# Mish MLP behind attention and soft MoE: the first chunks in another order, w_out tiles converted between the last expert products

## The chip, the cores and the metric

One core of one Trainium2 chip runs the whole program. The metric is the device time of one execution in microseconds; the kernel before takes 648.38 us, the median of three runs (647.77 to 648.62).

## The reference, cut to what matters

```python
x = attention(q, k, v, p)                      # [4608, 512], through 32 packed tokens per head
logits = x @ phi                               # soft MoE, 8 experts of 4 slots
slot_in = softmax(logits, 0).T @ x
slot_out[e] = relu(slot_in[e] @ w1[e]) @ w2[e] # 32 slots x 512
x = softmax(logits, 1) @ slot_out              # [4608, 512]
h = x @ w_in                                   # w_in [512, 2048]
out = (h * tanh(softplus(h))) @ w_out          # Mish; w_out [2048, 512]
```

Since x of the last layer is C @ slot_out, with C of 4608 x 32, the kernel never forms x: it forms slot_out @ w_in (32 x 2048, called MS) and then h = C @ MS.

## The kernel before, in words

Three stages follow each other: attention, the eight experts (weights streamed from HBM), and the MLP. The change lies where the experts end and the MLP begins, some 217 to 275 us after the start.

The helper names: `so` is the PSUM bank that collects the expert products; `ex_o(7, ...)` (L1009) adds those of the last expert. Its transpose `SOT` (128 x 4 x 32) is built through `so_sb` (two half copies, VectorE L1393 and ScalarE L1401) and `sot_ps` (L1394 to L1410) and copied out at L1414.

w_in and w_out arrive as 64-bit numbers and are converted on chip. For each of 16 `w_out` tiles of 128 x 512: `cz(k)` is a ScalarE pass over the high words (L280 or L282) into a `w64` buffer (four of them in turn), `cu(k)` two VectorE passes for the first four tiles (L286 and L289) and three for the others (L286, L289, L293). The tile is then split in two halves for the fast matmul format: `whi`, a rounding copy on ScalarE (L300 or L1183), and `wlo`, the rest, by a subtraction: on GpSimd for tiles 0 to 3 (`cw`, L301), on VectorE for tiles 4 to 15 (`cl`, L1184). Their loads wait in SyncE's queue (L174), in the order of a list made by `plan()`; a load into a ring slot waits until the slot's last user is done.

MS is made in four column groups of 512: `emit_mp(n)` multiplies SOT by a quarter of w_in (L1146) and copies the product to `msb` (L1149); `emit_mr(n)` repeats it over the four partition groups with one matmul (L1154), copies it to MS on an engine named in the call (L1156) and subtracts on VectorE, for partitions 64 to 127, what the rounded copy already holds (L1157). That subtraction reads the PSUM tile of the matmul once more. In the kernel before the tiles of `emit_mp` and `emit_mr` come from the pools `ps_x` (three banks) and `ps_so` (one).

The MLP goes over token blocks n of 256 and chunks c of 512 hidden columns. For a step (n, c): `emit_h(n, c, z)`, z = 0 and 1, makes half of h by two matmuls (L1199) into a tile of the pool `ps_h`, and ScalarE applies Mish (L1204). `emit_c` makes `gh` (rounding copy, ScalarE L1223) and `gl` (rest, VectorE L1224). `emit_o` issues 24 matmuls (L1317): 12 into a bank X for the first 128 tokens, and 12 into a bank Y; each dozen is gh by whi, gh by wlo, gl by whi, four each. Between the dozens it calls `mid`, which issues `emit_h` of the step after next. Column group c of MS serves chunk c. The first eight steps alternate two blocks: (0,0), (1,0), (0,1), (1,1), (0,2), (1,2), (0,3), (1,3).

`ps_h` has two buffers of two banks each, given out in turn, and a new tile may be written when the users of the tile that had the buffer are done:

```python
ps_h = hp_ctx.enter_context(tc.tile_pool(name="ps_h", bufs=2, space=PSUM, reuse_waits="tile"))
hp = ps_h.tile([128, 2, 512], F32, name="h3", tag="hp")[:, 0]      # in emit_h, one for each z
```

Nothing is scheduled by a planner here: each engine works through its instructions in the order in which the program text issues them, so a waiting instruction holds up all behind it on its engine. In the loop, step i issues, in this order: `emit_c` of step i+1; `emit_o` with `mid` in its middle; `cl` of two tiles, `cu` of the next two, `cz` of the two after those.

Of the kernel before, what the change touches and what calls it, by code (L numbers as in the profile page):

```python
# [19 lines left out]
def kernel(  # L20
# [264 lines left out]
    def cv_u(nm, i, name, dst, z, tv, fold):  # L285
        nc.vector.tensor_scalar(out=tv[:, :, 0], in0=tv[:, :, 0], scalar1=29, scalar2=None, op0=ALU.logical_shift_right)  # L286

    def cv_m(nm, i, name, dst, z, tv, fold):
        nc.vector.scalar_tensor_tensor(  # L289
            out=z if fold else tv[:, :, 1], in0=z, scalar=3, in1=tv[:, :, 0], op0=ALU.logical_shift_left, op1=ALU.bitwise_or,  # L290
        )
        if not fold:
            nc.vector.scalar_tensor_tensor(  # L293
                out=z, in0=z, scalar=-(2 ** 31), in1=tv[:, :, 1], op0=ALU.bitwise_and, op1=ALU.bitwise_or,
            )
        done(*name)

    def cv_w(nm, ft, name, w, z, tv, fold):

        nc.scalar.copy(out=whi[:, ft], in_=w)  # L300
        nc.gpsimd.tensor_tensor(out=wlo[:, ft], in0=w, in1=whi[:, ft].bitcast(F32), op=ALU.subtract)  # L301

    bgq = []

# [670 lines left out]
    def warm(n):  # L975

        if n:
            ps = ps_x.tile([128, 512], F32, name="warm", tag="x")
        for _ in range(n):
            nc.tensor.matmul(ps[:, 0:256], lhsT=ident, rhs=win[0][:, 0:256], start=True, stop=True)  # L980
# [28 lines left out]
    def ex_o(e, n=FT1, w=0, lo=0):  # L1009
        h1T = ex[e][1]  # L1010
        for ft in range(lo, n):
            g = ft % 4
            nc.tensor.matmul(
                so[32 * g:32 * g + 32], lhsT=h1T[:, ft], rhs=take("w2", e, ft // 2)[:, (ft % 2) * DM:(ft % 2 + 1) * DM],
                start=(e == 0 and ft < 4), stop=(e == E - 1 and ft >= n - 4),
            )
            if ft % 2:
                done("w2", e, ft // 2)
                if ft < n - 1:
                    warm(w)  # L1020
# [98 lines left out]
    ex_x(7)  # L1119
    ex_o(6)  # L1120
    combine_t(Lc[1], 7)
    warm(2)
    ex_o(7, FT1 - 2, 1)
    zero_c = two.tile([1, 128], F32, name="zero_c", tag="Lr")
    nc.gpsimd.memset(zero_c, 0.0)
    late_w = {}
# [8 lines left out]
    def ps_m():  # L1135
        np[0] += 1
        return ps_x.tile([128, 512], F32, name="mp", tag="x") if np[0] % 4 else ps_so.tile([128, 512], F32, name="so")

    def emit_mp(n, copy, i=0, w=512):

        mp = ps_m()
        if not i:
            msb[n] = t2.tile([128, 512], F32, name="msb", tag="msb")
        for kt in range(4):
            c = 512 * (kt % 2) + i
            nc.tensor.matmul(  # L1146
                mp[32 * kt:32 * kt + 32, 0:w], lhsT=SOT[:, kt], rhs=win[2 * n + kt // 2][:, c:c + w], start=True, stop=True,
            )
        copy(out=msb[n][:, i:i + w], in_=mp[:, 0:w])  # L1149

    def emit_mr(n, copy, i=0, w=512):

        mr = ps_m()
        nc.tensor.matmul(mr[:, 0:w], lhsT=idrep, rhs=msb[n][:, i:i + w], start=True, stop=True)  # L1154
        dst = MS[:, 512 * n + i:512 * n + i + w]
        copy(out=dst, in_=mr[:, 0:w])  # L1156
        nc.vector.tensor_tensor(out=dst[64:128], in0=mr[64:128, 0:w], in1=dst[64:128].bitcast(F32), op=ALU.subtract)  # L1157
# [13 lines left out]
    def cz(k):  # L1171
        late_w[k] = cv_z(*AFTER[E - 1, 1][k], fold=k < 4)
# [2 lines left out]
        cv_u(*late_w[k])  # L1175
        cv_m(*late_w[k])

    def cw(k):
        cv_w(*late_w[k])

    def cl(k):
        w, ft = late_w[k][3], late_w[k][1]
        nc.scalar.copy(out=whi[:, ft], in_=w)  # L1183
        nc.vector.tensor_tensor(out=wlo[:, ft], in0=w, in1=whi[:, ft].bitcast(F32), op=ALU.subtract)  # L1184

    R = {}

# [30 lines left out]
    def emit_c(n, c):  # L1218

        s, S = blk.pop(("m", n, c))  # L1220
        gh, gl = (wg.tile([128, 1024], F32, name=x, tag="wg").bitcast(F32R).rearrange("p (f n) -> p f n", f=4) for x in ("gh", "gl"))
        if S is None:
            nc.scalar.copy(out=gh, in_=s)  # L1223
            nc.vector.tensor_tensor(out=gl, in0=s, in1=gh.bitcast(F32), op=ALU.subtract)  # L1224
            blk["g", n, c] = gh, gl
            return
        Sh, Sl = (g2.tile([128, 1024], F32, name=x, tag=x, bufs=2).bitcast(F32R).rearrange("p (k f n) -> p k f n", k=4, f=2) for x in ("Sh", "Sl"))
        blocks = ((slice(0, 4), slice(0, 128)), (slice(2, 4), slice(128, 256)))
        for f, t in blocks:
            nc.scalar.copy(out=gh[:, f, t], in_=s[:, f, t])  # L1230
        nc.scalar.copy(out=Sh, in_=S)  # L1231
        for f, t in blocks:
            nc.vector.tensor_tensor(out=gl[:, f, t], in0=s[:, f, t], in1=gh[:, f, t].bitcast(F32), op=ALU.subtract)  # L1233
        nc.vector.tensor_tensor(out=Sl, in0=S, in1=Sh.bitcast(F32), op=ALU.subtract)  # L1234
        blk["g", n, c] = gh, gl, Sh, Sl
# [124 lines left out]
    def emit_store(n):  # L1360
# [24 lines left out]
        else:  # L1385
            for tt in range(2):
                for z in range(2):
                    b = 4 * (n - TB // 2) + 2 * tt + z
                    for j in range(2):
                        p0 = 64 * z + 32 * j  # L1390
                        (nc.scalar if n == NBLK - 1 and j else nc.sync).dma_start(out=rows(b)[:, 16 + j], in_=osb[p0:p0 + 32, tt])

    nc.vector.tensor_copy(out=so_sb[:, 0:256], in_=so[:, 0:256])  # L1393
    nc.tensor.matmul(sot_ps.rearrange("p k m -> p (k m)"), lhsT=zero_c, rhs=zero_c, start=True, stop=False)  # L1394
    for kt in range(4):
        i = 0 + 128 * kt
# [2 lines left out]
            start=False, stop=False,  # L1399
        )  # L1400
    nc.scalar.copy(out=so_sb[:, 256:512], in_=so[:, 256:512])  # L1401
    cz(0)
    for kt in range(4):
        nc.tensor.matmul(sot_ps[:, kt], lhsT=so_sb[:, 128 * kt:128 * kt + 128], rhs=ids, start=False, stop=False)
    for kt in range(4):
# [3 lines left out]
            start=False, stop=(kt == 3),  # L1409
        )  # L1410
    done("w2", E - 1, 3)
    cv_u(*late_w[0])
    cz(1)
    nc.vector.tensor_copy(out=SOT, in_=sot_ps)  # L1414
    ep.close()
    W3 = arena.tile([128, 1024 * RW], F32R, name="W3", tag="AW")
# [8 lines left out]
        i = (0 if x == "osb" else 2048) + 1024 * turn[x]  # L1425
        return AY[:, i:i + 1024]

    cv_m(*late_w[0])
    emit_mp(0, nc.scalar.copy, 0, 256)
    emit_mp(0, nc.vector.tensor_copy, 256, 256)  # L1430
    cv_u(*late_w[1])
    emit_mp(1, nc.scalar.copy, 0, 256)
    cz(2)
    emit_mr(0, nc.scalar.copy, 0, 256)
    emit_mr(0, nc.scalar.copy, 256, 256)
    emit_mp(1, nc.vector.tensor_copy, 256, 256)
    cz(3)
    nc.scalar.activation(out=tab_c, in_=half_c, func=AF.Mish)
    cv_m(*late_w[1])
    cv_u(*late_w[2])  # L1440
    emit_mp(2, nc.scalar.copy)
    emit_mr(1, nc.vector.tensor_copy)
    cv_m(*late_w[2])
    emit_h(0, 0, 0)
    cw(0)
    cw(1)
    emit_h(0, 0, 1)
    cu(3)
    cw(2)
    emit_c(0, 0)  # L1450
    emit_mp(3, nc.vector.tensor_copy)
    emit_mr(2, nc.scalar.copy)
    cw(3)
    cz(4)
    emit_h(1, 0, 0)
    emit_h(1, 0, 1)
    cu(4)
    emit_mr(3, nc.scalar.copy)
    cz(5)
    cz(6)  # L1460
    cu(5)
    cz(7)
    R["X"], R["Y"] = (ps_x.tile([128, 512], F32, name="o3", tag="x") for _ in range(2))
    R["X1"], R["Y1"] = ps_x.tile([128, 512], F32, name="o3", tag="x"), ps_so.tile([128, 512], F32, name="so")
    work = {}
    for i, (n, c) in enumerate(steps):
        if i == 6:
            next(work[3])
            wp.close()
            g2 = ctx.enter_context(tc.tile_pool(name="g2", bufs=2, reuse_waits="tile"))  # L1470
            hp_ctx.close()
            ps_b = ctx.enter_context(tc.tile_pool(name="ps_b", bufs=1, space=PSUM, reuse_waits="tile"))
            R.update({x: ps_b.tile([128, 512], F32, name="o3", tag=x) for x in "ZV"}, U=R["X1"], W=R["Y1"])
        nx = steps[i + 2] if i + 2 < len(steps) else None
        last_s = fast(n, c) and c == ORDER[n][-1]

        def mid(z):
            if z == 0 and last_s:
                nc.scalar.copy(out=quads(n)[1], in_=rq("Z"))
            if z == 1 and last_s:  # L1480
                add(quads(n)[2], quads(n)[1], rq("V"))
            if z in (0, 2) and nx:
                emit_h(*nx, z // 2)

        if i + 1 < len(steps):
            emit_c(*steps[i + 1])
        emit_o(n, c, mid)
        early = c == ORDER[n][-1] and n + 1 in PLAIN and not fast(n + 1, ORDER[n + 1][0])
        if early and last_s:
            emit_store(n)  # L1490
        if nx:
            emit_m(*nx)
        if i < 6:
            for k in (2 * i + 4, 2 * i + 5):
                cl(k)
            for k in (2 * i + 6, 2 * i + 7):
                if k < NL:
                    cu(k)
            for k in (2 * i + 8, 2 * i + 9):
                if k < NL:  # L1500
                    cz(k)
        if i == 4:
            work.update({c: build_t(c, [late_w[k][3] for k in range(12, 16)] if c == 3 else None) for c in range(4)})
        if c == ORDER[n][-1] and not (early and last_s):
            emit_store(n)
        for x in TW.get(i, ""):
            next(work[int(x)])
# [31 lines left out]
```

## Time and profile before

| | |
|---|---|
| median of 3 runs | 648.38 us |
| the profiled execution's own time | 644.71 us |
| its span | 642.9 us |
| TensorE matmul busy | 611.3 us, 95% |
| VectorE, ScalarE, GpSimd busy | 501.1, 337.8, 55.2 us |
| mean granted TensorE clock | 0.989 |
| read from HBM, written | 79.2 MB, 9.4 MB |

The span is what the trace covers; the profiled execution's own time is 1.8 us more, for what lies around it. The median of the runs is 3.7 us above the profiled execution. A matmul's end is modelled, and matmuls overlap in the records, so the starts of TensorE's instructions say more than their sums. Times in the rows are counted from the start of the span.

### The profile page before, as it was taken

How to read it: one execution, taken by the hardware profiler on the slowest of the kernel's cores; microseconds unless marked ns; L12 is line 12 of the kernel's file. 1: busy time of each engine (PE TensorE's matmuls, PEld its weight loads, DVE VectorE, ACT ScalarE, POOL GpSimd, SP SyncE). 2: the span in 40 equal slices, each digit the busy share in tenths (PEclk: the TensorE clock that was granted, in tenths of full speed). 3: DMA queues.
4: the chain of work that ended last, by engine and by line, in shares of the span. 5: the costliest groups of instructions: out<-in, count | busy, mean ns of one | idle time of the engine just before them, and what ended most of it. 6: DMA issues, size and time to landing. Idle time of an engine off the chain costs nothing.

```text
span 642.9 us, 14422 instructions
## 1 busy us (share of the span) xinstructions
PE 611.3 (95%) x5874; PEld 528.6 (82%) x5874; DVE 501.1 (78%) x997; ACT 337.8 (53%) x681; POOL 55.2 (9%) x78
## 2 busy tenths in 40 slices
PE   7899999998998969999999999999999999999996
PEld 5777777776344548888899999999999999999996
DVE  5998888887564398988779987788778877887883
ACT  3345555646334367655456555555555555555551
POOL 5122222121020030010000000000000000000000
PEclk9899999998999979999999999999999999999999
DMA  8988955999999960020110110111011101110111
GB/s 283 344 292 292 343 174 199 405 413 396 360 410 412 412 223 1 1 53 14 33 34 2 34 34 2 35 34 34 2 34 34 34 2 34 34 34 2 34 34 34
DMA packets 42354, 89.61 MB, mean 139 GB/s; under 512 B 10928, under 2 KB 19248, under 8 KB 42288
## 3 DMA queue, kind: packets, MB, share of 16 engines
q1 hardware_dynamic: 41840, 88.36, 38.8%
q8 instruction: 46, 0.75, 0.5%
q10 hardware_dynamic: 192, 0.26, 0.2%
q14 instruction: 20, 0.16, 0.1%
q0 software_dynamic: 256, 0.07, 0.0%
HBM read 79.23 MB, written 9.44 MB: 138 GB/s over the span
## 4 chain that ended last, share of the span: by engine, by line
PE 65%; DVE 18%; DMA 8%; ACT 5%; issue 1%; SPq 1%; DVEq 0%; POOL 0%; ACTq 0%; POOLq 0%
PE o L1317 39%; PE so L1317 14%; DMA AW<-in_moe_w_dram 6%; PE h L1199 5%; DVE kT L335 4%; DVE A L507 1%; DMA r_wo<-in_moe_w_out_dram 1%; DVE mx L506 1%; PE s L487 1%; DVE AY L1358 1%; DVE S L1215 1%; DVE sm L522 1%; DVE nmx L383 1%; PE s L820 1%; ACT AT L545 1%
## 5 line engine op out<-in xcount | busy, mean ns | idle before, releaser
L1317 PE MATMUL o<-W,gh 128*128 128x256 f32 (+1 forms) x888 | 159.4, 306 | 0.5 <-DVE AY L1358 0.5
L1317 PEld LDWEIGHTS o<-W,gh 128*128 128x128 f32 x888 | 129.7, 190 | 10.0 <-issue 1.9
L1230 ACT CAST gh<-AY 128x512 fp32r<-128x512 f32 x116 | 53.8, 511 | 109.1 <-PE o L1317 109.1
L1204 ACT ACTIVATE AY<-h 128x512 f32<-128x512 f32 x132 | 77.1, 594 | 37.4 <-PE h L1199 36.0
L1317 PE MATMUL o<-W,gl 128*128 128x256 f32 (+1 forms) x444 | 94.3, 302 | 0.0
L1233 DVE TENSOR_TENSOR gl<-AY,gh 128x512 fp32r<-128x512 f32 x116 | 59.4, 553 | 33.0 <-ACT gh L1230 33.0
L1234 DVE TENSOR_TENSOR Sl<-S,Sh 128x1024 fp32r<-128x1024 f32 x58 | 70.9, 1223 | 10.4 <-ACT Sh L1231 9.0
L1317 PEld LDWEIGHTS o<-W,gl 128*128 128x128 f32 x444 | 70.7, 188 | 4.5
L1317 PE MATMUL o<-T,Sh 128*128 128x256 f32 x464 | 73.9, 281 | 0.4 <-DVE AY L1358 0.4
L1231 ACT CAST Sh<-S 128x1024 fp32r<-128x1024 f32 x58 | 60.8, 1049 | 5.6 <-DVE S L1215 4.3
L1317 PEld LDWEIGHTS o<-T,Sh 128*128 128x128 f32 x464 | 62.8, 189 | 0.6 <-DVE AY L1358 0.6
L1215 DVE TENSOR_TENSOR S<-AY 128x256 f32<-128x256 f32 x116 | 48.7, 420 | 9.9 <-ACT AY L1204 9.9
L1199 PE MATMUL h<-CS,W 128*128 128x256 f32 x288 | 55.7, 284 | 0.0
L1317 PE MATMUL o<-T,Sl 128*128 128x256 f32 x232 | 46.6, 282 | 0.0
L1199 PEld LDWEIGHTS h<-CS,W 128*128 128x128 f32 x288 | 43.9, 188 | 2.2 <-issue 0.7
L1358 DVE TENSOR_TENSOR AY<-AY,o 128x256 f32<-128x256 f32 x86 | 33.0, 417 | 9.4 <-PE o L1317 6.4
L1317 PE MATMUL so<-T,Sh 128*128 128x256 f32 (+1 forms) x232 | 38.7, 289 | 0.4 <-DVE AY L1358 0.4
L373 PE MATMUL s<-kT,win 128*128 128x288 f32 x128 | 34.7, 416 | 2.4 <-ACT win L385 2.3
L1317 PEld LDWEIGHTS o<-T,Sl 128*128 128x128 f32 x232 | 35.8, 190 | 0.0
L487 PE MATMUL s<-win,qT 128*128 128x128 f32 x256 | 33.7, 287 | 1.9 <-ACT win L353 1.9
L487 PEld LDWEIGHTS s<-win,qT 128*128 128x128 f32 x256 | 31.4, 200 | 2.8 <-issue 2.0
L1317 PEld LDWEIGHTS so<-T,Sh 128*128 128x128 f32 x232 | 32.5, 190 | 1.2 <-issue 0.6
(282 smaller groups left out, 1039.5 us busy)
## 6 DMA issues: line engine op xcount, KB each, us to landing
AW<-in_moe_w_dram SPq DMA_DIRECT2D x45, 512.0 KB, 10.2
r_wo<-in_moe_w_out_dram SPq DMA_DIRECT2D x16, 512.0 KB, 9.0
out_dram<-AY SPq DMA_DIRECT2D x64, 128.0 KB, 2.1
r_wi<-in_moe_w_in_dram SPq DMA_DIRECT2D x13, 512.0 KB, 8.8
AW<-in_q_dram SPq DMA_DIRECT2D x11, 576.0 KB, 5.2
AW<-in_k_dram SPq DMA_DIRECT2D x9, 576.0 KB, 7.3
AW<-in_v_dram SPq DMA_DIRECT2D x40, 128.0 KB, 5.6
AC<-in_moe_w_dram SPq DMA_DIRECT2D x10, 512.0 KB, 9.1
```

What stands on the lines that cost most here:

```text
L335: nc.vector.transpose(out=T[:, dh, main].rearrange("p (i r a) -> p a i r" if nm == "k" else "p (i a r) -> p a i r", i=4, a=4,), in_=x[:, 0 ...
L373: nc.tensor.matmul(ps[:, n, 0:288], lhsT=pBD[b % 2][:, hq, dh], rhs=kT[:, dh, 288 * n:288 * n + 288], start=(dh == 0), stop=(dh == 1),)
L487: nc.tensor.matmul(ps[:, k - lo], lhsT=d["qT", hq][:, dh, 64 + 128 * i:192 + 128 * i], rhs=ppBD[b % 2][:, hq, dh], start=(dh == 0), stop=( ...
L1199: nc.tensor.matmul(hp[:, 256 * f:256 * f + 256], lhsT=MS[:, 128 * ft:128 * ft + 128], rhs=CS[:, 256 * n:256 * n + 256], start=True, stop=True,
L1204: nc.scalar.activation(out=s, in_=hp.rearrange("p (f n) -> p f n", f=2), func=AF.Mish)
L1215: nc.vector.tensor_tensor(out=S[:, k], in0=x, in1=y, op=op)
L1230: nc.scalar.copy(out=gh[:, f, t], in_=s[:, f, t])
L1231: nc.scalar.copy(out=Sh, in_=S)
L1233: nc.vector.tensor_tensor(out=gl[:, f, t], in0=s[:, f, t], in1=gh[:, f, t].bitcast(F32), op=ALU.subtract)
L1234: nc.vector.tensor_tensor(out=Sl, in0=S, in1=Sh.bitcast(F32), op=ALU.subtract)
L1317: nc.tensor.matmul(o, lhsT=lhsT, rhs=rhs, start=first, stop=stop)
L1358: add = lambda o, x, y: nc.vector.tensor_tensor(out=o, in0=x, in1=y, op=ALU.add)
```

## The change

`warm(2)` and the call of `ex_o` for the last expert are taken from their place, and the call stands later, without the warming matmuls between its pairs, behind the conversion of w_out tile 0. The conversions of tiles 0 to 2 and `cz(3)` stand between the steps that build SOT, and the load of ScalarE's Mish table with them. `cw`, GpSimd's subtraction, is gone: `cwh(k)` is its ScalarE copy and `cwl(k)` the subtraction, on VectorE. Only column group 0 of MS is made ahead of the first h; two single matmuls (`fill`) into a spare tile stand between its parts. Group 1's product is made before the loop; its spreading and groups 2 and 3 are issued in `mid` of steps 0, 1 and 2, into the two banks of one `ps_h` tile for each step. In step 0, `emit_c` of step 1 and `emit_h` of step 2 stand behind `emit_o`. `cu(5)`, `cz(6)` and `cz(7)` move into step 0.

```diff
-    def cv_w(nm, ft, name, w, z, tv, fold):
-        nc.scalar.copy(out=whi[:, ft], in_=w)
-        nc.gpsimd.tensor_tensor(out=wlo[:, ft], in0=w, in1=whi[:, ft].bitcast(F32), op=ALU.subtract)
...
-    warm(2)
-    ex_o(7, FT1 - 2, 1)
...
-        mp = ps_m()
+        mp = ps_m() if n < 2 else hp_m[n]
...
-        mr = ps_m()
+        mr = ps_m() if n < 1 else hp_m[n + 4]
...
+    def cwh(k):
+        nc.scalar.copy(out=whi[:, late_w[k][1]], in_=late_w[k][3])
+    def cwl(k):
+        w, ft = late_w[k][3], late_w[k][1]
+        nc.vector.tensor_tensor(out=wlo[:, ft], in0=w, in1=whi[:, ft].bitcast(F32), op=ALU.subtract)
...
+    cz(0)
+    cu(0)
+    ex_o(7, FT1 - 2, 0)
+    cz(1)
     nc.vector.tensor_copy(out=so_sb[:, 0:256], in_=so[:, 0:256])
+    cu(1)
...
     nc.scalar.copy(out=so_sb[:, 256:512], in_=so[:, 256:512])
-    cz(0)
+    cz(2)
+    cu(2)
+    cz(3)
+    nc.scalar.activation(out=tab_c, in_=half_c, func=AF.Mish)
...
+    def fill(ps, n):
+        for _ in range(n):
+            nc.tensor.matmul(ps[:, 0:256], lhsT=ident, rhs=win[0][:, 0:256], start=True, stop=True)
+    cwh(0)
     emit_mp(0, nc.scalar.copy, 0, 256)
     emit_mp(0, nc.vector.tensor_copy, 256, 256)
+    cwh(1)
+    spare = ps_h.tile([128, 2, 512], F32, name="spare", tag="hp")
+    fill(spare[:, 0], 1)
     emit_mr(0, nc.scalar.copy, 0, 256)
     emit_mr(0, nc.scalar.copy, 256, 256)
+    fill(spare[:, 1], 1)
+    cwh(2)
     emit_h(0, 0, 0)
     emit_h(0, 0, 1)
     cu(3)
...
+    for f in (0, 2):
+        nc.scalar.copy(out=gh[:, f:f + 2], in_=s0[:, f:f + 2])
+    cwh(3)
+    for k in range(4):
+        cwl(k)
+    nc.vector.tensor_tensor(out=gl, in0=s0, in1=gh.bitcast(F32), op=ALU.subtract)
+    emit_mp(1, nc.scalar.copy)
     emit_h(1, 0, 0)
     emit_h(1, 0, 1)
+    cz(4)
     cu(4)
     cz(5)
...
-            if z in (0, 2) and nx:
+            if z == 0 and i < 3:
+                t = ps_h.tile([128, 2, 512], F32, name="mr", tag="hp")
+                hp_m.update({i + 5: t[:, 0], i + 2: t[:, 1]})
+                emit_mr(i + 1, nc.scalar.copy)
+                if i < 2:
+                    emit_mp(i + 2, nc.scalar.copy)
+            if z in (0, 2) and nx and i:
                 emit_h(*nx, z // 2)
-        if i + 1 < len(steps):
+        if i + 1 < len(steps) and i:
             emit_c(*steps[i + 1])
         emit_o(n, c, mid)
+        if not i:
+            emit_c(*steps[1])
+            for z in range(2):
+                emit_h(*nx, z)
+            for k in (5, 6):
+                cu(k) if k < 6 else cz(k)
+            cz(7)
```

## Rows read from the trace of the kernel before

**Rows 1.** Windows: busy us (instructions) of each engine, granted clock, DMA share, GB/s.

```profile
234.00:240.00 6.00, 5.88 (x12) 3.98 (x13) 5.46 (x10) 3.62 (x6) 0.47 (x1) 0.51 0.43 159
252.00:258.00 6.00, 6.00 (x29) 4.95 (x28) 5.82 (x10) 4.34 (x7) 0.00 (x0) 1.00 0.00 0
```

**Rows 2.** Timeline of TensorE: start, us, engine, line, operation, tiles, shape, count.

```profile
220.56 1.50 PE L1146 MATMUL mp<-win,SOT 128*32 128x256 f32 x24 [0.38 <-DVE SOT L1414]
...
226.22 1.06 PE L1146 MATMUL mp<-AY,SOT 128*32 128x512 f32 x8
227.22 1.12 PE L1154 MATMUL mp<-msb,idrep 128*128 128x512 f32 x2
...
234.12 2.07 PE L1154 MATMUL mp<-msb,idrep 128*128 128x512 f32 x2 [5.30 <-DVE msb L1149]
235.20 4.40 PE L1317 MATMUL o<-W,gh 128*128 128x512 f32 x8
...
240.54 0.64 PE L1199 MATMUL h<-CS,W 128*128 128x256 f32 x4
...
249.88 2.03 PE L1317 MATMUL o<-W,gh 128*128 128x512 f32 x8
...
252.68 0.62 PE L1199 MATMUL h<-CS,W 128*128 128x256 f32 x4
...
274.12 2.03 PE L1317 MATMUL o<-W,gh 128*128 128x512 f32 x8
```

**Rows 3.** The chain of waits, 227 to 232 us: start, us, what.

```profile
227.31 1.80 DVE w L289
...
230.64 1.57 DVE w L289
```

**Rows 4.** Windows of half a microsecond, TensorE alone: busy, granted clock, DMA.

```profile
233.00:233.50 0.50, 0.00 (x0) 0.51 0.82 82
239.50:240.00 0.50, 0.50 (x3) 0.66 0.27 107
```

**Rows 5.** Loads of w_out: the first and the fourth issue, and the time to landing.

```profile
206.90 0.33 SPq L174 DMA_DIRECT2D r_wo<-in_moe_w_out_dram  x1
210.81 0.33 SPq L174 DMA_DIRECT2D r_wo<-in_moe_w_out_dram  x1
...
r_wo<-in_moe_w_out_dram SPq DMA_DIRECT2D x1, 512.0 KB, 8.9
```

**Rows 6.** Timeline of ScalarE.

```profile
217.80 1.22 ACT L280 ACTIVATE w<-r_wo 128x512 f32<-128x512 f32 x2
221.26 0.37 ACT L1149 COPY msb<-mp 128x256 f32<-128x256 f32 x1 [2.25 <-PE mp L1146]
224.21 1.28 ACT L1438 ACT_TABLE_LOAD   x1
...
253.10 1.09 ACT L1204 ACTIVATE s<-h 128x512 f32<-128x512 f32 x2 [1.47 <-PE h L1199]
254.07 1.14 ACT L1183 CAST W<-w 128x512 fp32r<-128x512 f32 x2
...
256.65 1.04 ACT L1223 CAST gh<-s 128x1024 fp32r<-128x1024 f32 x1
```

**Rows 7.** Timeline of VectorE.

```profile
220.21 0.29 DVE L1414 COPY SOT<-sot_ps 128x128 f32<-128x128 f32 x1 [2.44 <-PE sot_ps L1407]
...
236.88 0.69 DVE L1157 TENSOR_TENSOR W<-mp,W 64x512 fp32r<-64x512 f32 x1
...
251.68 0.42 DVE L286 TENSOR_SCALAR r_wo<-r_wo 128x512 int32<-128x512 int32 x1
252.13 0.69 DVE L289 SCALAR_TENSOR_TENSOR r_wo<-w,r_wo 128x512 int32<-128x512 int32 x1
...
253.47 1.22 DVE L1224 TENSOR_TENSOR gl<-s,gh 128x1024 fp32r<-128x1024 f32 x1
254.73 1.29 DVE L1184 TENSOR_TENSOR W<-w,W 128x512 fp32r<-128x512 f32 x2
```

More of the change, by code (lines that the diff above doesn't have):

```diff
@@ L1137, in ps_m @@
         return ps_x.tile([128, 512], F32, name="mp", tag="x") if np[0] % 4 else ps_so.tile([128, 512], F32, name="so")
+    hp_m = {}
     def emit_mp(n, copy, i=0, w=512):
-        mp = ps_m()
+        mp = ps_m() if n < 2 else hp_m[n]
         if not i:
@@ L1176, in cu @@
         cv_m(*late_w[k])
-    def cw(k):
-        cv_w(*late_w[k])
+    def cwh(k):
[3 more added lines that the diff above has]
+        nc.vector.tensor_tensor(out=wlo[:, ft], in0=w, in1=whi[:, ft].bitcast(F32), op=ALU.subtract)
     def cl(k):
-        w, ft = late_w[k][3], late_w[k][1]
-        nc.scalar.copy(out=whi[:, ft], in_=w)
-        nc.vector.tensor_tensor(out=wlo[:, ft], in0=w, in1=whi[:, ft].bitcast(F32), op=ALU.subtract)
+        cwh(k)
+        cwl(k)
     R = {}
@@ L1411 @@
     done("w2", E - 1, 3)
-    cv_u(*late_w[0])
-    cz(1)
     nc.vector.tensor_copy(out=SOT, in_=sot_ps)
@@ L1426, in two_of @@
         return AY[:, i:i + 1024]
-    cv_m(*late_w[0])
+    def fill(ps, n):
+        for _ in range(n):
+            nc.tensor.matmul(ps[:, 0:256], lhsT=ident, rhs=win[0][:, 0:256], start=True, stop=True)
+    cwh(0)
     emit_mp(0, nc.scalar.copy, 0, 256)
     emit_mp(0, nc.vector.tensor_copy, 256, 256)
-    cv_u(*late_w[1])
-    emit_mp(1, nc.scalar.copy, 0, 256)
-    cz(2)
+    cwh(1)
+    spare = ps_h.tile([128, 2, 512], F32, name="spare", tag="hp")
+    fill(spare[:, 0], 1)
     emit_mr(0, nc.scalar.copy, 0, 256)
     emit_mr(0, nc.scalar.copy, 256, 256)
[L1436 to L1443, printed above, removed]
+    fill(spare[:, 1], 1)
+    cwh(2)
     emit_h(0, 0, 0)
-    cw(0)
-    cw(1)
     emit_h(0, 0, 1)
     cu(3)
[L1449 to L1454, printed above, removed]
+    s0 = blk.pop(("m", 0, 0))[0]
+    gh, gl = blk["g", 0, 0] = [
+        wg.tile([128, 1024], F32, name=x, tag="wg").bitcast(F32R).rearrange("p (f n) -> p f n", f=4) for x in ("gh", "gl")
+    ]
+    for f in (0, 2):
+        nc.scalar.copy(out=gh[:, f:f + 2], in_=s0[:, f:f + 2])
+    cwh(3)
+    for k in range(4):
+        cwl(k)
+    nc.vector.tensor_tensor(out=gl, in0=s0, in1=gh.bitcast(F32), op=ALU.subtract)
+    emit_mp(1, nc.scalar.copy)
     emit_h(1, 0, 0)
     emit_h(1, 0, 1)
+    cz(4)
     cu(4)
-    emit_mr(3, nc.scalar.copy)
     cz(5)
-    cz(6)
-    cu(5)
-    cz(7)
     R["X"], R["Y"] = (ps_x.tile([128, 512], F32, name="o3", tag="x") for _ in range(2))
```

## The prediction

> **What bounds the kernel now.** I read four views in this order: windows, TensorE's timeline, the chain of waits, and the queues of ScalarE and VectorE. The windows say where there is something to win. From 252 to 258 us TensorE is busy all the time at full clock and VectorE 5.82 of 6 us: the steps of the MLP run at TensorE's pace, and from the step that begins at 249.88 to the one at 274.12, four steps, each takes 6.06 us [rows 1, 2]. Between 234 and 240 the clock is 0.51 [rows 1]. TensorE's timeline shows why: ahead of 234.12 it stood idle for 5.30 us, for VectorE's copy of the last MS product; the clock fell at 233.0, in the gap, and came back near 239.7 [rows 2, 4]. So the first dozen of `o` took from 235.20 to 240.54, 5.34 us, where a step of 6.06 less 0.46 for its four h matmuls gives 2.80 for a dozen [rows 2]. The chain of waits says why that copy was late: VectorE's conversion passes took 1.80 and 1.57 us there, where the same pass takes 0.69 later [rows 3, 7]; GpSimd's subtractions ran beside them.
>
> At stake are therefore some 8 us between 229 and 240: 5.3 idle and 2.5 of half clock.
>
> **The change, part by part.** *Up to SOT: nothing gained.* The last expert's products end some 2.3 us sooner without their warming matmuls, but `cu(0)` now stands ahead of the copy of `so` on VectorE, and `cz(1)` ahead of its second half on ScalarE. Tile 0 lands at 206.90 + 8.9 = 215.8, tile 1 1.3 later (between issues 1 and 4 lie 3.9 us [rows 5]). `cz(0)` ends at 216.5, the two-pass `cu(0)` at 217.3, the copies at 217.7 and 218.2; the sixteen small matmuls then end as before, and SOT stands at 220.5, as now (220.21 + 0.29 [rows 7]). TensorE waits from 215.9 to 218.2.
>
> *From SOT to the first chunk: 10 us gained.* ScalarE's queue now has `cz(3)`, the table load and `cwh(0)` ahead of the first MS copy. Tile 3 lands at 210.81 + 8.9 = 219.7; 0.57 for `cz` (two take 1.22, so one 0.57 start to start with the tail of the last), 1.4 for the table and its dummy, 0.52 for `cwh` give 222.2 [rows 5, 6]. SOT's product would have been ready at 220.55 + 0.70 (220.56 to 221.26 [rows 2, 6]), so the tile's landing and the table load, hidden before, cost 1 us here. Copy, spreading matmul, copy and subtraction, 0.37 + 0.70 + 0.37 + 0.42, and 0.5 for the second half, bring VectorE to 224.6. Then in its queue: `cu(3)` 1.1, four `cwl` at 0.62 (two take 1.29, with 1.20 to the next), gl 1.22: 229.4 [rows 7]. ScalarE has two Mish halves and two half copies of gh (1.0 and 0.9) behind h at 224.7, which ends at 226.6; then `cwh(3)` ends at 227.2 [rows 6], and so the first `o` starts at 227.3; the four products with gl start at 229.45 and the dozen ends at 230.4. In the kernel before it ended at 240.54 [rows 2]: 10.15 sooner. The loss of GpSimd is in this: VectorE takes over 4 x 0.62 = 2.5 and is rid of 1.11 + 0.88 in the two passes above, and of more in what lay between them.
>
> *Moved, not removed.* At 240.54 all of MS was made. Now two products and three spreadings of 512 columns are still to come, each about 0.95 on TensorE (226.22 to 227.22 [rows 2]), in a stage where TensorE has no idle time to hide them: 5 x 0.95 = 4.75 given back. Leaves 5.4.
>
> *The new wait, in step 1.* `mid` of step 1 takes a `ps_h` tile for `emit_mr(2)` and `emit_mp(3)`; `emit_h` z=0 takes the other buffer, and z=1 the first again. Its matmuls must wait until VectorE's subtraction has read the spreading out of that bank; behind them on TensorE stand the second dozen and all else. No row shows such a wait, since the spreadings had other pools; so I follow both queues. TensorE from 230.4: 0.95 + 0.95, a dozen 2.80, h 0.47, a dozen 2.80, 0.95 + 0.95, half an h 0.24: z=1 is up at 240.5. VectorE from 229.4, with that subtraction last in its order: `cu(4)` 1.8 (251.68 to 253.47 [rows 7]), the subtraction of group 1 0.62, gl 1.2, `cu(5)` 1.8, `cwl` 4 and 5 1.24, `cu` 6 and 7 3.6, gl 1.2, the subtraction 0.7: 12.2 of work, 241.6 at the earliest, a wait of 1.1. It is not free of waits itself: for group 1's spreading (ends at 230.4 + 1.12 [rows 2], copied in 0.6: 1.0 idle), for gh (ScalarE comes to it after the msb copy at 233.1, and takes 1.04: 1.35 idle), and for `cwh(4)` (ScalarE does Mish after h at 235.6, 1.0, then `cz` 6 and 7, 1.14, then the copy 0.62: 1.25 idle) [rows 6]. With these 3.6 the subtraction ends at 245.15, and TensorE waits **4.7 us**. I take that value, since each of the three is a queue in fixed order with measured lengths; the range keeps 1.1.
>
> *The same in step 2.* VectorE is then ready, and what remains is the path within the step: spreading 1.12, copy 0.6, subtraction 0.7 against 0.95 + 0.24 of TensorE's own: **1.45 us**. Step 0 has no such wait, as its h stands behind the second dozen.
>
> *Sum at full clock:* 10.15 - 4.75 - 4.7 - 1.45 = -0.75: step (0,3) begins at 274.9 instead of 274.12. From there the order is unchanged, VectorE is 3 us ahead of need, as before (a gl that ends at 254.7 is needed at 249.88 + 6.06 + 1.87, behind eight matmuls [rows 2, 7]), and the shift stays to the end. `cu` 5, `cz` 6 and 7 move within queues that wait anyway. The loads of tiles 11 to 15 can be issued sooner, since their slots are freed sooner; SyncE's queue and GpSimd's hold nothing else that waits.
>
> *The clock.* A gap of 5.30 us let it fall, and it stayed low for 5.6 us after work began again [rows 2, 4]. The new gap of 4.7 is nearly as long. Before, this cost 5.34 - 2.80 = 2.54 on the first dozen; I take the same for the second dozen of step 1. The bounds are 0 (no fall) and 5.1 (a second stretch, after the gaps at 216 or in step 2). The Trainium skill, page TensorE: Matmul & The Clock Gate, part 1, What's actually happening, says that the throttled state is the default and that activity lifts it. By that rule the gap costs what the rows' gap cost; with a clock that stays up through it the sum would be 0.75 alone.
>
> **Sum:** 0.75 + 2.54 = 3.3 us slower. The profiled execution would take 644.71 + 3.3 = 648.0; the median of the runs lies 3.67 above that execution, so it would be 648.38 + 3.3 = **651.7 us**.
>
> **The rivals.** *A, the forecast:* wait and one slow stretch; with the wait from 4.0 to 5.2 and the clock's cost from 1.7 to 3.4, 650.2 to 653.2. Chance 0.54.
>
> *B, the clock stays up:* 648.38 + 0.8 = 649.2. For it: the gap is 0.6 shorter than the one seen, and the clock fell only 4.2 us into that one. Chance 0.15.
>
> *C, faster: no wait in step 1*, because the pool gives z=1 another buffer than the spreading's, or the subtraction is out before. Then MS's columns 2 and 3 cost only their 4.75. The next limit is VectorE: `cwl` 6 and 7 and their copies come 1.9 us late for step (0,1). 5.4 - 1.9 = 3.5 gained: 644.9. It decides at the point where z=1's matmuls start directly behind z=0's. Against it: in a step before, all four h matmuls are through in 0.62 us, while the Mish that frees z=0's buffer ends at 253.7 [rows 2, 6], so neighbours get different buffers and the turn comes back to the spreading's. The Trainium skill, page PSUM: Partial Sum Buffer, section PSUM bank collisions raise a hardware error, asks for semaphores by bank, so that no write may pass a reader of its bank; no row here shows it, and by it C has only the timing left. Chance 0.17.
>
> *D, two slow stretches or more*, as TensorE works with gaps from 216 to 227 too: 0.75 + 5.1, 654.2. Chance 0.14.
>
> **How the numbers follow.** A measurement of this kernel can tell about 0.2%, 1.3 us, from no change. A and D are slower by more, 0.68; B is within, 0.15; C faster, 0.17. The range from 646.5 to 654.5 holds A and B, most of D and C's upper edge, where the wait is near its lower bound of 1.1 and the clock stays.
>
> **What would show it.** In the profile after: no GpSimd subtraction and VectorE's passes at 0.69; the first `o` near 227 with its gl products at 229.5; the chain of waits with z=1's h of step 1 waiting for VectorE's subtraction, some 4 to 5 us, and a shorter one in step 2; the clock at half from about 243 to 250; step (0,3) at 276 to 278. If h of step 1 does not wait, or the steps run at 6.06 from 231 on, the prediction is wrong at the new wait; if the wait is there and the clock is not, at the last term.

## The result, and the profile after

The change makes the kernel slower: 655.38 us, the median of four runs (654.20 to 656.63), against 648.08 us of the kernel before in four runs on the same chip. The ratio is 1.0115, 95% interval [1.0091, 1.0139], so 7.5 us of 648. Forecast were 3.3 us and 651.7; the range ended at 654.5. The direction was right, the size not.

The spans differ by 11.1 us (642.9 and 654.0), but 2.1 of them arise ahead of the change: the last matmul of the combine (`cp`, operand `Lr`) starts at 211.48 before and at 213.58 after, though both kernels are the same up to there (first the row before, then the one after):

```profile
211.48 0.22 PE L1065 MATMUL cp<-ident,Lr 64*32 64x64 f32 x1
213.58 0.22 PE L1060 MATMUL cp<-ident,Lr 64*32 64x64 f32 x1
```

So I count from that matmul, "the mark", to the end of the span: 431.42 us before, 440.42 after, 9.0 more. In a second execution of the changed kernel it was 438.96, 7.5 more. Two executions of one program thus differ by 1.5 us here, and a smaller difference between two totals shows nothing by itself.

Windows of the profiled execution after, chosen where the clock changes; the columns are those of [rows 1].

```profile
212.00:219.00 7.00, 5.79 (x65) 2.79 (x56) 0.82 (x3) 1.38 (x3) 0.00 (x0) 1.00 1.04 417
219.00:230.00 11.00, 9.80 (x44) 7.68 (x44) 4.84 (x12) 6.43 (x13) 0.00 (x0) 0.53 1.02 409
230.00:250.00 20.00, 14.34 (x66) 8.48 (x65) 14.47 (x23) 13.26 (x23) 0.00 (x0) 1.00 0.29 103
250.00:257.00 7.00, 5.13 (x17) 2.81 (x18) 2.31 (x3) 2.80 (x5) 0.00 (x0) 0.53 0.00 0
257.00:286.00 29.00, 28.06 (x127) 22.50 (x126) 25.71 (x41) 17.17 (x28) 0.00 (x0) 1.00 0.00 1
```

Half clock stands in two rows, not in one; GpSimd does nothing in them any more; and between 230 and 250, at full clock, TensorE is busy for only 14.34 of 20 us. What it waited for there, TensorE's timeline shows (`mr` names the two-bank tile that spreading and product share; `mr<-msb` is a spreading, `mr<-AY` a product).

```profile
219.81 1.91 PE L1410 MATMUL sot_ps<-ids,so_sb 128*128 128x32 f32 x8 [1.84 <-DVE so_sb L1395]
...
231.74 2.37 PE L1315 MATMUL o<-W,gh 128*128 128x512 f32 x8
...
235.57 1.02 PE L1149 MATMUL mr<-msb,idrep 128*128 128x512 f32 x2
238.00 1.06 PE L1141 MATMUL mr<-AY,SOT 128*32 128x512 f32 x8 [1.40 <-DVE W L1152]
...
245.16 1.02 PE L1149 MATMUL mr<-msb,idrep 128*128 128x512 f32 x2
251.87 1.94 PE L1141 MATMUL mr<-AY,SOT 128*32 128x512 f32 x8 [5.69 <-DVE W L1152]
253.74 1.57 PE L1197 MATMUL h<-CS,W 128*128 128x256 f32 x4
255.10 2.98 PE L1315 MATMUL so<-W,gh 128*128 128x512 f32 x8
...
258.86 2.03 PE L1315 MATMUL o<-W,gh 128*128 128x512 f32 x8
...
263.85 0.50 PE L1197 MATMUL h<-CS,W 128*128 128x256 f32 x2 [0.94 <-ACT s L1202]
...
285.17 2.03 PE L1315 MATMUL o<-W,gh 128*128 128x512 f32 x8
```

The reader is to see who waits in the two rows of L1141: not h, but the *product* of the next column group, and both times for VectorE's subtraction L1152, which reads the *spreading* of the group before. The two matmuls write different banks of one tile. After the second wait, of 5.69 us, the clock is at half, and from the product at 251.87 to step 2's first dozen at 258.86 pass 6.99 us. Step (0,3) begins at 285.17, 11.05 later than in [rows 2]; from there to the end nothing more is lost or won (11.1 in the spans).

Why the subtraction is late, VectorE's timeline shows:

```profile
240.70 1.23 DVE L1222 TENSOR_TENSOR gl<-s,gh 128x1024 fp32r<-128x1024 f32 x1 [2.75 <-ACT gh L1221]
...
245.07 1.29 DVE L1178 TENSOR_TENSOR W<-w,W 128x512 fp32r<-128x512 f32 x2 [1.35 <-ACT W L1174]
...
249.87 1.22 DVE L1222 TENSOR_TENSOR gl<-s,gh 128x1024 fp32r<-128x1024 f32 x1
251.12 0.69 DVE L1152 TENSOR_TENSOR W<-mr,W 64x512 fp32r<-64x512 f32 x1
256.48 0.69 DVE L1178 TENSOR_TENSOR W<-w,W 128x512 fp32r<-128x512 f32 x1 [4.66 <-ACT W L1174]
```

It stands last in VectorE's queue of that step, behind two conversions and gl. It also needs ScalarE's copy of the spreading, and that stands late in ScalarE's queue:

```profile
247.91 0.59 ACT L1151 CAST W<-mr 128x512 fp32r<-128x512 f32 x1
```

The copy is out at 248.50 and the subtraction starts at 251.12, so some 2.6 us of the wait are VectorE's order; the rest had passed before the copy was out. VectorE idles 2.75 and 1.35 us ahead of the subtraction and 4.66 behind it: it is not short of time. The order of the queues is the trouble, together with who waits for the last entry.

### The profile page after: what moved, and what is told of

It reads as the page before. It is cut to its first block, busy times and chain, and to the rows that moved or that the text cites. A ratio compares the mean times of both kernels' runs of the same rounds, so it can differ in the third digit from the quotient of the medians.

```text
span 654.0 us, 14390 instructions
## 1 busy us (share of the span) xinstructions
PE 616.4 (94%) x5862; PEld 531.0 (81%) x5862; DVE 499.7 (76%) x998; ACT 339.4 (52%) x684; POOL 49.2 (8%) x74
## 4 chain that ended last, share of the span: by engine, by line
PE 70%; DVE 14%; DMA 9%; ACT 5%; issue 1%; SPq 1%; DVEq 0%; POOL 0%; ACTq 0%; POOLq 0%
PE o L1315 40%; PE so L1315 14%; DMA AW<-in_moe_w_dram 6%; PE h L1197 5%; DVE kT L330 3%; PE s L482 2%; PE s L368 2%; DMA r_wo<-in_moe_w_out_dram 1%; DVE A L502 1%; DVE mx L501 1%; DVE AY L1356 1%; DMA AC<-in_q_dram 1%; DVE nmx L378 1%; ACT AT L540 1%; DMA AC<-in_k_dram 1%
## 5 line engine op out<-in xcount | busy, mean ns | idle before, releaser
L1315 PE MATMUL o<-W,gh 128*128 128x256 f32 (+1 forms) x888 | 157.5, 304 | 0.5 <-DVE AY L1356 0.5
L1315 PEld LDWEIGHTS o<-W,gh 128*128 128x128 f32 x888 | 128.3, 188 | 9.8 <-issue 1.7
L1197 PE MATMUL h<-CS,W 128*128 128x256 f32 x288 | 57.3, 289 | 0.9 <-ACT s L1202 0.9
L368 PE MATMUL s<-kT,win 128*128 128x288 f32 x128 | 36.1, 428 | 2.5 <-ACT win L380 2.4
```

The lines of the kernel that those rows point to most:

```text
L368: nc.tensor.matmul(ps[:, n, 0:288], lhsT=pBD[b % 2][:, hq, dh], rhs=kT[:, dh, 288 * n:288 * n + 288], start=(dh == 0), stop=(dh == 1),)
L1197: nc.tensor.matmul(hp[:, 256 * f:256 * f + 256], lhsT=MS[:, 128 * ft:128 * ft + 128], rhs=CS[:, 256 * n:256 * n + 256], start=True, stop=True,
L1315: nc.tensor.matmul(o, lhsT=lhsT, rhs=rhs, start=first, stop=stop)
```

## The experiments

From the two traces I took this theory: (a) what the program makes wait is the two-bank tile as a whole, so a product into one bank waits for the readers of the spreading in the other; (b) the gap ahead of SOT (1.84 us) and the one in step 1 (5.69 us) each bring a stretch of half clock, and these cost on top. Rivals: VectorE is simply overloaded now that GpSimd's subtractions are its own; or the clock only lies beside waits that end late anyway. In the table "mark to end" comes from one profiled execution, the ratio from timed runs against the kernel before on the same chip.

| | ratio to before | mark to end, us |
|---|---|---|
| before | 1 | 431.42 |
| changed kernel | 1.0115 [1.0091, 1.0139] | 440.42 |
| changed kernel again | 1.0111 [1.0075, 1.0147] | 438.96 |
| product ahead of spreading | 1.0066 [1.0042, 1.0091] | 435.06 |
| first gap filled | 1.0088 [1.0056, 1.0120] | 437.51 |
| own banks | 1.0015 [0.9995, 1.0036] | 431.92 |
| four subtractions on GpSimd | 1.0099 [1.0062, 1.0136] | 440.67 |
| second gap filled | 1.0099 [1.0071, 1.0127] | 437.51 |
| both gaps filled | 1.0052 [1.0028, 1.0076] | 435.61 |
| own banks, first gap filled, `cu(3)` sooner | 0.9959 [0.9934, 0.9984] | 429.31 |

Product first, first gap, own banks and GpSimd ran beside one set of runs of the kernel before (645.48 us, 17 runs), the four others below the changed kernel's first row beside another (646.26 us, 30 runs).

**Product ahead of spreading** in `mid`: the same two matmul groups in the same tile, exchanged.

```diff
-                emit_mr(i + 1, nc.scalar.copy)
                 if i < 2:
                     emit_mp(i + 2, nc.scalar.copy)
+                emit_mr(i + 1, nc.scalar.copy)
```

> In mid of steps 0 and 1 the product of the next column group is issued ahead of the spreading, in the same two-bank tile. Theory T (the second bank waits because the whole tile waits for VectorE's subtraction out of the first): the wait of 1.4 us in step 0 goes and the product of group 3 no longer stands behind the 5.7 us wait; what is left is the h matmul z=1 of step 1 waiting for the subtraction, some 2 to 4 us on top of its own. Some 2.5 us faster than the changed kernel, so 652.9 us. Rival (the product waits for something else that VectorE is late with, such as the buffer it is copied to): the product still waits 1.4 us in step 0 and the time stays at 655.4.

Measured: TensorE's timeline now shows the products without a wait, and the spreadings waiting, for ScalarE's copy of the product out of the *other* bank:

```profile
238.62 1.12 PE L1149 MATMUL mr<-msb,idrep 128*128 128x512 f32 x2 [0.71 <-ACT msb L1144]
...
249.06 1.13 PE L1149 MATMUL mr<-msb,idrep 128*128 128x512 f32 x2 [2.24 <-ACT msb L1144]
...
251.36 0.79 PE L1197 MATMUL h<-CS,W 128*128 128x256 f32 x2 [0.94 <-ACT s L1202]
```

The wait turns round with the order, as it must if the tile is the unit. The sum of the waits on the tile falls from 7.09 to 2.95 us; mark to end falls by 3.9 against the second execution of the changed kernel, 5.4 against the first, and by the ratios (1.0111 and 1.0066) the gain is 2.9 us of 646. That is near the 2.5 us expected. What is left came out otherwise: expected was z=1's h of step 1 waiting 2 to 4 us for the subtraction, but it waits 0.94 us for Mish and starts at 251.36, before the subtraction does (251.62). Both stretches of half clock are still there.

**Own banks.** Groups 1 to 3 use the single banks X and Y of step 1 (`X1`, `Y1`), which are empty in step 0, and all are issued in the middle of step 0's `emit_o` or behind it; no matmul shares a tile with another's readers or with h.

```diff
-            if z == 0 and i < 3:
-                t = ps_h.tile([128, 2, 512], F32, name="mr", tag="hp")
-                hp_m.update({i + 5: t[:, 0], i + 2: t[:, 1]})
...
+            if z == 0 and i < 1:
+                hp_m.update({5: R["X1"], 2: R["Y1"], 3: R["X1"], 6: R["Y1"], 7: R["X1"]})
+                emit_mr(1, nc.scalar.copy)
+                emit_mp(2, nc.scalar.copy)
...
+            emit_mp(3, nc.scalar.copy)
+            emit_mr(2, nc.scalar.copy)
             for z in range(2):
                 emit_h(*nx, z)
+            emit_mr(3, nc.scalar.copy)
```

> Column groups 1 to 3 go through the two banks that step 1 will accumulate in (they are empty in step 0), all issued in step 0: spreading 1 and product 2 in its middle, product 3 and spreadings 2 and 3 behind its second dozen. No tile is shared with h. Theory T (the waits for VectorE's subtraction in steps 0 to 2, 1.4, 5.7 and 0.9 us, and the slow stretch behind the long one are what the groups cost): 7.5 us faster than the changed kernel, so level with the kernel before, 647 to 649.5; one slow stretch is left, the one before the first chunk. Rival (VectorE has too much to do without GpSimd and is late whatever the tiles): at most 3 us faster, 652.4 or more.

Measured: level with the kernel before, 431.92 from the mark, 8.5 less than the changed kernel's first execution and 7.0 less than its second. The list of what TensorE waited for (line, who, total, times, longest), first of the changed kernel from 213 to 286 us, then of this one:

```profile
PE mr L1141 <- DVE W L1152: 7.1, 2, 5.7
PE sot_ps L1410 <- DVE so_sb L1395: 1.8, 1, 1.8
PE h L1197 <- ACT s L1202: 0.9, 1, 0.9
...
```

```profile
PE sot_ps L1410 <- DVE so_sb L1395: 1.8, 1, 1.8
PE o L1315 <- DVE W L1152: 1.5, 1, 1.5
PE o L1315 <- ACT W L1174: 0.5, 1, 0.5
...
```

The 7.1 us of the products are gone, and with them the second slow stretch: of the windows from 226 to 280 none is below full clock, while the first stretch is still there. A new wait of 1.5 us stands in its place, of step 1's dozen on the subtraction that empties its own bank. The windows:

```profile
219.00:226.00 7.00, 6.62 (x35) 4.83 (x35) 2.06 (x5) 4.49 (x8) 0.00 (x0) 0.53 1.03 407
226.00:280.00 54.00, 51.19 (x234) 36.65 (x233) 46.76 (x77) 36.90 (x65) 0.00 (x0) 1.00 0.16 61
```

Spreading and product of step 0:

```profile
232.85 1.02 PE L1149 MATMUL o<-msb,idrep 128*128 128x512 f32 x2
233.80 1.06 PE L1141 MATMUL so<-AY,SOT 128*32 128x512 f32 x8
```

In step 0 the two stand where they stood in the changed kernel, in the same order, and only the banks are others: the product now starts 0.95 us behind the spreading, not 2.43. Together with the exchange above, this settles (a). For the 5.69 us of step 1 the edit is not as clean, since groups 2 and 3 are also issued sooner.

**Four subtractions on GpSimd**, as in the kernel before:

```diff
-        nc.vector.tensor_tensor(out=wlo[:, ft], in0=w, in1=whi[:, ft].bitcast(F32), op=ALU.subtract)
+        (nc.gpsimd if k < 4 else nc.vector).tensor_tensor(out=wlo[:, ft], in0=w, in1=whi[:, ft].bitcast(F32), op=ALU.subtract)
```

> The subtractions for w_out tiles 0 to 3 go back to GpSimd, all else as in the changed kernel. Theory T (VectorE's extra 2.5 us are not what costs): the products with wlo wait up to 1 us longer for GpSimd's 1.46 us each, so 0 to 1.5 us slower than the changed kernel, 655.4 to 657. Rival (taking GpSimd away overloads VectorE and its lateness in step 1 comes from there): 2 us or more faster, 653.4 or less.

Measured: nothing won, 440.67 from the mark. The ratio is 1.0 us below the changed kernel's, with intervals that overlap, between what the theory (0 to 1.5 us more) and the rival (2 us or more less) expected; it does not decide. The trace does: the wait in step 1 is as long, and one on GpSimd comes in:

```profile
232.62 0.50 PE L1315 MATMUL o<-W,gh 128*128 128x512 f32 x1 [0.69 <-POOL W L1178]
...
250.30 1.94 PE L1141 MATMUL mr<-AY,SOT 128*32 128x512 f32 x8 [5.80 <-DVE W L1152]
```

The four subtractions on VectorE are not the cause. The run also shows what GpSimd's subtractions do to VectorE, as in [rows 3]: beside them the second pass over tile 3 (L289, from 228.03) takes 1.66 us, where it takes 0.69 in the changed kernel.

**First gap filled**: four matmuls, whose result nobody reads, in the wait ahead of SOT.

```diff
+    hold = ps_h.tile([128, 2, 512], F32, name="hold", tag="hp")
+    for _ in range(4):
+        nc.tensor.matmul(hold[:, 0, 0:256], lhsT=ident, rhs=win[0][:, 0:256], start=True, stop=True)
```

> Four spare matmuls of 256 columns fill the gap of 1.8 us in which TensorE waits for the copy of the expert sum. Theory T (the slow stretch from 219.7 to 229.9 us comes from that gap and costs some 3 us up to the first chunk): the clock stays up until the wait in step 1, the first o starts 2 us sooner and its gl products 3 us sooner; 3 to 4 us faster than the changed kernel, 651.5 to 652.5. Rival (landings, ScalarE and VectorE set that path, the clock only stretches matmuls that have time): within 1 us of 655.4.

Measured: 437.51, 2.9 less than the first execution of the changed kernel, 1.45 less than the second; by the ratios 1.5 to 1.7 us, with intervals that overlap, where 3 to 4 were expected. Windows of this kernel, and its first `o`:

```profile
212.00:230.00 18.00, 16.26 (x124) 9.91 (x116) 8.89 (x18) 11.47 (x23) 0.00 (x0) 1.00 1.03 412
230.00:245.00 15.00, 10.63 (x46) 6.48 (x44) 9.68 (x16) 9.54 (x16) 0.00 (x0) 1.00 0.26 101
245.00:253.00 8.00, 4.84 (x16) 2.61 (x17) 3.27 (x5) 2.55 (x5) 0.00 (x0) 0.59 0.01 2
```

```profile
228.16 2.22 PE L1315 MATMUL o<-W,gh 128*128 128x512 f32 x8
```

The first slow stretch is gone, the second stands. The first `o` starts at 228.16, 15.37 us behind the mark (212.79); without the fill it was 18.16 (213.58 to 231.74), and 17.32 in the second execution. So the fill gives 2.0 to 2.8 us up to there. That is the clock: tile 3's conversion, behind which ScalarE's copies stand, starts 8.25 us behind the mark here and 8.27 and 8.42 without the fill. The total gains less than that against the second execution, since the slow stretch that is left costs 0.5 us more here: from step 1's product to step 2's first dozen pass 6.88 us (248.16 to 255.04), against 6.37 there.

**Second gap filled**, after that **both**, with the changed kernel once more as their control:

```diff
                 emit_mr(i + 1, nc.scalar.copy)
+                for _ in range(44 if i == 1 else 0):
+                    nc.tensor.matmul(R["Y1"][:, 0:256], lhsT=MS[:, 0:128], rhs=CS[:, 0:256], start=True, stop=True)
                 if i < 2:
                     emit_mp(i + 2, nc.scalar.copy)
```

> The changed kernel once more, nothing edited but a comment, so that the fills below are compared with it on one chip. Its own trace gave 440.4 us from the last combine to the end, two stretches of low granted clock and waits of 1.40 and 5.69 us of the product matmuls on the subtraction. Expected by every theory: the same again, 440 to 441 us from the last combine to the end, 1.009 to 1.014 of the kernel before. If it came out at another ratio, the later differences would be taken against this run and not against the first.

> The changed kernel with 44 spare matmuls (256 columns each, their result read by nobody) on TensorE ahead of step 1's product matmul, in the 5.69 us that it waits for the subtraction. Theory (the wait of the two-bank tile costs twice: its own length, and the low clock that follows it, 250.4 to 257.2 us): the product matmul still begins at the same time behind the subtraction, but the clock stays up there, and the work behind it is some 2.4 us shorter: mark to end 438.0 against 440.4 (436.5 to 439), ratio about 0.0037 below the changed kernel's. Rival (the second low stretch lies beside waits that end late in any case): the clock stays up and the time is the same, mark to end 440 or over.

> Both gaps filled: the four spare matmuls behind the last spreading ahead of step 0 and the 44 in step 1's wait. Theory (two causes that add: waits on a tile of two banks at full clock, and two stretches at low clock): the granted clock shows no low stretch from 212 us to the end of step 2; what remains over the kernel before is the waits, 1.40 and 5.69 us less what the new order gains, by my reckoning at full clock +4.2 us: mark to end 435.6 (434.5 to 437), ratio 1.0055 to 1.0075. Rival (the waits alone carry the loss, the clock only lies beside them): 439 or over. Rival on the other side (the clock alone is the loss): level with the kernel before, 431 to 432.5.

The control came out 1.5 us shorter from the mark than the first execution, at the same ratio. In half-microsecond windows its low stretches last from 219.2 to 226.0 and from 246.5 to 253.3; in the first execution they lasted from 219.7 to 229.9 and from 250.4 to 257.2, so the first one was 3.4 us longer with nothing different in the program. Differences below are against the control.

Second gap filled, TensorE's timeline, and behind it two rows of the control:

```profile
242.63 5.83 PE L1490 MATMUL so<-CS,W 128*128 128x256 f32 x44
248.88 1.07 PE L1141 MATMUL mr<-AY,SOT 128*32 128x512 f32 x8 [0.42 <-DVE W L1152]
...
253.80 2.03 PE L1315 MATMUL o<-W,gh 128*128 128x512 f32 x8
```

```profile
249.35 1.93 PE L1141 MATMUL mr<-AY,SOT 128*32 128x512 f32 x8 [5.68 <-DVE W L1152]
...
255.72 2.03 PE L1315 MATMUL o<-W,gh 128*128 128x512 f32 x8
```

The product still begins when the subtraction is out, 6.71 us behind the spreading (242.17 to 248.88), as in the changed kernel (245.16 to 251.87, 6.71 too); but from it to step 2's first dozen pass 4.92 us, not 6.99 (6.37 in the control, 249.35 to 255.72). That is the price of half clock behind the gap: 1.45 to 2.07 us. The low stretch lasts 6.8 us in both executions of the changed kernel; in the first, 1.5 us of it lie in the wait, in the control 2.85, so the control has less of it left to pay for. Mark to end is 1.45 shorter (expected were 2.4). By the ratios alone (1.0099 and 1.0111) this run is not told from the control; the trace tells it. With both gaps filled no window from 212 to 280 us is below full clock (columns: window, its length, TensorE busy and instructions, granted clock, DMA share, GB/s):

```profile
212.00:280.00 68.00, 62.78 (x338) 1.00 0.35 136
```

The waits remain, and mark to end is 435.61: 3.35 less than the control, and 4.2 more than the kernel before. This settles (b), and the two fills add: 1.95 us up to the first `o` and 1.45 behind step 1's wait, against 3.35 for both. The 4.2 us that are left are, by difference and not by a run of their own, what the waits cost net of what the new order gains.

**A version that beats both**: own banks and the first gap filled; the last spreading moves to the end of step 1 into a tile of its own, and `cu(3)` directly behind the copy of SOT.

```diff
+    cu(3)
...
-    cu(3)
...
+                hp_m.update({5: R["X1"], 2: R["Y1"], 3: R["X1"], 6: R["Y1"]})
...
+        if i == 1:
+            hp_m[7] = ps_h.tile([128, 2, 512], F32, name="mr", tag="hp")[:, 0]
+            emit_mr(3, nc.scalar.copy)
```

> A version that may beat both: the changed kernel with the four spare matmuls ahead of step 0, groups 1 to 3 each in the single banks of step 0 (no tile shared with the hidden product; the last spreading in a tile of its own at the end of step 1), and group 3's conversion directly behind the copy of the spread counts. Own banks alone gave 431.9 us from the last combine to the end with one low stretch left, and the fill alone took 2.9 us off the changed kernel. Theory (the two causes add): 428.5 to 429.5, ratio 0.995 to 0.998 of the kernel before. Rival (the low stretch that is left with own banks lies beside VectorE's and ScalarE's work and is worth nothing there): 431 to 432, level with the kernel before. A third way: a new wait of the first chunk's matmuls on the conversions of w_out takes part of it, 430 to 431.

Measured: 643.60 us against 646.26, ratio 0.9959 [0.9934, 0.9984]; 429.31 from the mark, 2.1 less than before. TensorE's timeline:

```profile
232.11 1.07 PE L1141 MATMUL so<-AY,SOT 128*32 128x512 f32 x8
...
245.08 1.13 PE L1149 MATMUL mr<-msb,idrep 128*128 128x512 f32 x2 [0.33 <-ACT s L1202]
...
247.40 1.48 PE L1315 MATMUL o<-W,gh 128*128 128x512 f32 x4 [0.74 <-ACT W L1174]
249.09 1.10 PE L1315 MATMUL o<-W,gh 128*128 128x512 f32 x2 [0.22 <-DVE W L1178]
```

and VectorE's:

```profile
232.84 0.69 DVE L1152 TENSOR_TENSOR W<-o,W 64x512 fp32r<-64x512 f32 x1 [0.90 <-ACT W L1151]
```

The product that waited 1.40 us in the changed kernel starts at 232.11 and is still running when VectorE reads the spreading, 232.84 on, out of another bank. Step 0's wait in the changed kernel was one that the work did not need. Of the 1.3 us of small waits shown, 0.96 are for conversions of w_out and 0.33 for Mish. How much of the 2.1 us the moved `cu(3)` gives was not run apart; up to the first `o` it gives nothing (15.40 us behind the mark, 15.37 with the fill alone).

## Why the prediction was wrong

Times below count the trace after from the mark as the kernel before has it, so they are 2.1 us less than in that trace. Step (0,3) was forecast at 274.9 plus 2.54 for the clock, 277.44; it came at 283.07, 5.6 later. The parts of those 5.6 are +3.1, +1.6, +1.2 and -0.3, step by step. In the second execution it came 4.0 late (+2.1, +1.6, +0.7 and -0.3); with the 3.3 of the forecast that makes 7.3, and it is the one that fits the timed runs.

*"Up to SOT: nothing gained"* held to a few tenths up to the restart: the SOT transposes wait until 217.7 (forecast 218.2). But SOT stood at 221.7, forecast 220.5: by the step "the sixteen small matmuls then end as before", and they ran at half clock.

*"From SOT to the first chunk: 10 us gained"* was right in its mechanism: no GpSimd subtraction, VectorE's passes at 0.69 (0.42 in the short form) where [rows 3] had 1.80 and 1.57. With the clock held, the first `o` came 15.37 us behind the mark; the forecast had 15.82. Its dozen ended 19.09 us behind the mark (the next spreading starts at 231.88), forecast 18.92. In the changed kernel itself it ended at 233.5, forecast 230.4: **+3.1** (+2.1 in the second execution). This sum of queues was right; what was missing in it is the clock.

*"Moved, not removed"*, 4.75, was read too high. A product takes 1.0 us to the next start, but the prediction took a product's 0.95 for the spreadings too. A spreading with h behind it takes 0.46 in the changed kernel (261.65 to 262.11) and took 0.56 in the kernel before (227.22 [rows 2] to 227.78):

```profile
227.78 1.03 PE L1199 MATMUL h<-CS,W 128*128 128x256 f32 x4
```

Only with a product behind it, as in step 0 of the last kernel (231.16 to 232.11), is it 0.95. Step 2 has 0.5 us of this; in steps 0 and 1 the waits cover it.

*"The new wait, in step 1"* is **the step that failed in kind**. It said that z=1's h waits, since the turn of `ps_h` comes back to the spreading's bank, and that "Step 0 has no such wait". What waits is the next product, in the other bank of the same tile, and it is issued before any h; so step 0 waits as well, 1.40 us (**+1.6** with 0.2 of pauses between matmul groups). I had followed the tile's buffer round the pool and not asked what stands beside it in the same buffer. In step 1 the size was near, 5.69 against 4.7, and so was the reason: VectorE was 3.0 us late from the first chunk and idled 2.75 us for gh where 1.35 were forecast; TensorE came later too, by the 3.1 and 1.6. Step 1 altogether is **+1.2**: the wait 1.0 longer, 0.7 because h follows the product at once and z=1 waits for ScalarE's copy of that product too (with the second gap filled it starts 0.77 us behind z=0, where half an h is 0.24), the clock 0.5 less (below). Rival C's condition was partly met, z=1 in step 2 waits not for the subtraction but for Mish (it starts at 263.85, the subtraction ends at 264.02), and still nothing was won, since C too looked at h alone.

The Trainium skill, page PSUM — Partial Sum Buffer, section PSUM bank collisions raise a hardware error, asks for semaphores by bank and quadrant. By that rule product and spreading, in two banks, need not wait for each other, and the prediction used it only for h. The last kernel above agrees with the rule (writing one bank from 232.11, reading the other from 232.84); the program's waits in the changed kernel were wider than it.

*"The same in step 2"*, 1.45, is 1.23 by its own terms (2.42 less 1.19). It came for another reason: z=1 waits for Mish on ScalarE. It starts 1.74 us behind z=0 where half an h is 0.24, so 1.5 in all, of which the row shows 0.94 as idle. With the 0.5 us that the spreading is shorter and a tenth more of pauses, the step is **-0.3**.

*"The clock"* is **the second failed step**: one stretch at 2.54, where there were two. The one it named costs 1.45 to 2.07. The one it left out of the sum, ahead of SOT, is the 3.1 above (2.1 in the second execution). It stood among the bounds and as rival D, 5.1 for both; with both gaps filled the total is 4.8 us below the first execution and 3.35 below the second. So D named the right thing, at a price somewhat high, and its chance of 0.14 was too low; that its 654.2 is near the measured 655.4 is in part luck, as step 0's wait is not in it. The gap at 216 to 218 was in the forecast, and the warming matmuls that the change removes stood right ahead of it.

"Slower" came out for the reasons given: the gain at the first chunk is given back by moved work and by a wait on VectorE's last entry. At full clock, with both gaps filled, the loss was 4.2 where the prediction's sum was 0.75; the missing 3.4 are step 0's wait (1.6), step 1's (1.7) and tenths.

## What to carry to other kernels

When two matmul groups share a PSUM tile, look at what waits for the tile, not for the bank: in this program a writer of one bank waited for the reader of the other, in either order; single-bank tiles took away the 1.40 us of step 0, and with the groups also moved into step 0 all 7.1 us were gone. When work is removed from in front of TensorE, list every gap that this opens and price the clock behind each one, short ones too. And a reader that stands last in another engine's queue is no place to hang a matmul on, however idle that engine is.

## What the runs showed of the hardware that was not expected

The granted clock fell, at 219.7, in a gap of only 1.84 us (217.98 to 219.81), where the kernel before kept full clock for some 4.2 us of a gap of 5.30 [rows 2, 4]. TensorE had done the eight small matmuls of SOT just ahead of it. The clock then stayed at half for 6.8 us in one execution and for 10.2 in another of the same program. In the six traces with this gap unfilled it was 6.8 us in four (the control, product first, own banks, second gap filled) and 10.2 in two (the first execution, GpSimd). In the first execution of the changed kernel it stayed low with instructions running nearly all the time (columns: window, its length, TensorE busy and instructions, granted clock, DMA share, GB/s):

```profile
220.00:229.00 9.00, 8.62 (x41) 0.50 1.03 408
```

With the spare matmuls in that gap it stayed at full clock in all three kernels that had them. After the gap of step 1 it came back 4.0 us behind the restart in one execution of the changed kernel (249.35 to 253.3) and 5.3 in the other (251.87 to 257.2); in the kernel before it was 5.7 (234.12 to 239.84, by the clock of 0.66 in the last window of [rows 4]). The Trainium skill, page TensorE: Matmul & The Clock Gate, part 1, What's actually happening, says that the throttled state is the default and activity lifts it; the filled gaps agree, while the 9 us of the row above, with TensorE's records in 8.62 of them, passed at 0.50 all the same. Why the low stretch ahead of SOT lasts 6.8 us once and 10.2 another time, no run here shows.
